# Keys and queries in DRAM with their three parts side by side, read 48 rows at a time

## Chip, cores and metric

One NeuronCore of a Trainium2 chip runs the whole program. The metric is device time in microseconds (us) of one execution; three runs of the kernel before are given. The profile is one more execution, recorded by the hardware profiler.

## The reference

Two layers of an attention block and a dense block over 2048 rows of 512 features, in float32:

```python
B, S, D, H = 1, 2048, 512, 32        # head size 16; dense width F = 1792
def _A_ref(x, wqkv, wo):
    qkv = transpose((x @ wqkv).reshape(B, S, 3, H, Dh), 2, 0, 3, 1, 4)
    q, k, v = qkv[0], qkv[1], qkv[2]
    scores = einsum("bhqd,bhkd->bhqk", q, k) * (Dh ** -0.5)
    p = softmax(scores, axis=-1)
    return transpose(einsum("bhqk,bhkd->bhqd", p, v), 0, 2, 1, 3).reshape(B, S, D) @ wo
def _B_ref(x, w1, b1, w2):            # dense, Mish, dense
    h = einsum("bsd,df->bsf", x, w1) + b1
    return einsum("bsf,fd->bsd", h * tanh(softplus(h)), w2)
x = x + _A_ref(layernorm(x), wqkv, wo)
x = x + _B_ref(layernorm(x), w1, b1, w2)      # and both lines once more
```

## The kernel before

Every float32 number that goes into a matmul is carried as two float32r parts, a high one (`th`, index 0) and a low one (`tl`, index 1), and a product is three matmuls: high by high, high by low, low by high.

**Projections.** `qkv` (L470) goes through a list `order` of tiles (m, c): m is one of 8 blocks of 128 output rows (0 to 3 queries, 4 to 7 keys), c one of 4 chunks of 512 tokens. The tile is 12 matmuls (L164 to L166, or L159 for the first two) into a PSUM bank of the tag "s", of which there are three. `evict` (L488) then splits it: ScalarE writes the high part to the buffer `pt` (L151), VectorE the low part (L152), and one DMA issued on ScalarE's queue (L491) stores both parts, 512 KB, to the DRAM tensor `scr[m]`, laid out [part, row, token]. `pt` has the tag "raw" with three buffers. In layer 0 the tag is shared with freshly loaded weights. Values come after 22 tiles of queries and keys in layer 0 and after 16 in layer 1: `va` tiles, also in the PSUM tag "s", go through ScalarE to one half of `vst` (L537), and a DMA on SyncE's queue (SP, L538) stores them to `vscr`. Both halves are used in turn, so the third value tile waits for the first store.

**A head's operands.** Attention works on eight groups of four heads. A group's two `ks` and two `qs` buffers each hold two heads, at partitions 0 and 64. One head takes 48 rows, which make the three products in one matmul: for keys the 16 rows of the high part twice and those of the low part (`K_PARTS`), for queries high, low, high (`Q_PARTS`). Two further rows hold ones (keys, L244) and the negative row maximum (queries, L337). `prep_qk` (L232) fills the 48 rows with three DMAs of 16 rows each (L251), all on SP's queue, which issues in order. For group 0 it is called twice in `qkv`: for the columns 0 to 1535 when the third chunks of m = 0 and 4 are stored, and for the last 512 columns (the edge) when the fourth chunks are. For later groups it is a generator, which `run` (L420) advances by one DMA at each of the attention's steps, from the group before.

**Attention.** `run` interleaves score matmuls (`sp`, L355), exponentials on ScalarE (L357), products with the values (`pv`, L402), and, 22 steps ahead, the row maxima: matmuls `pm` and `pn` (L275) with VectorE reductions (L293, L308). The first maxima are laid between the value tiles (`some_max`, L479): `pm` takes two heads of the first buffers of `ks` and `qs`, `pn` one head each of the second ones. The order on each engine is settled when the program is built, partly by chains of dependences written in the code (`Order`, L85), elsewhere by a scheduler with a model of the times. An instruction that waits holds back all that stand behind it on its engine.

```python
KROWS = 48
K_PARTS = (0, 0, 1)
Q_PARTS = (0, 1, 0)
```

Of the kernel before, what the change touches and what calls it, by code (L numbers as in the profile page):

```python
# [10 lines left out]
F32 = mybir.dt.float32  # L11
F32R = mybir.dt.float32r
# [7 lines left out]
P = 128  # L20
S, D, H, DH, F = 2048, 512, 32, 16, 1792
NCH = 4
CW = S // NCH
# [10 lines left out]
KROWS = 48  # L34
MROWS = 50
HALF = 64
K_PARTS = (0, 0, 1)
Q_PARTS = (0, 1, 0)
CYCLE = "QvXXvQMXvvXM"
TAIL_START = "QvvRvv"  # L40
TAIL = "WQRvvv"
# [10 lines left out]
def kernel(ctx: ExitStack, tc: tile.TileContext, x, wqkv, wo, w1, b1, w2, out):  # L52
    nc = tc.nc
# [7 lines left out]
    dram = ctx.enter_context(tc.tile_pool(name="dram", bufs=1, space=DRAM))  # L61
# [12 lines left out]
    def b8(shape, dt, name):  # L74
        return blk.tile(shape, dt, tag="blk", name=name)
# [3 lines left out]
    def pbank(tag, name):  # L79
        return ps.tile([P, 512], F32, tag=tag, name=name, bufs=PS_BUFS[tag])  # L80
# [69 lines left out]
    def split_psum(hi, lo, src):  # L150
        nc.scalar.activation(hi, src, AF.Copy)  # L151
        nc.vector.tensor_tensor(lo, src, hi.bitcast(F32), op=ALU.subtract)  # L152
# [8 lines left out]
    def mm3(acc, pairs, first=True, last=True, pe=lambda ins: ins):  # L161
        n = len(pairs)
        for i, (ah, al, bh, bl) in enumerate(pairs):
            pe(nc.tensor.matmul(acc, ah, bh, start=first and i == 0, stop=False))  # L164
            pe(nc.tensor.matmul(acc, ah, bl, start=False, stop=False))  # L165
            pe(nc.tensor.matmul(acc, al, bh, start=False, stop=last and i == n - 1))  # L166
# [49 lines left out]
    class Attention:  # L216
# [15 lines left out]
        def prep_qk(self, g, first=0, last=S):  # L232
            l = self.l
            if g not in self.qk:
                self.qk[g] = [
                    [b8([P, S], F32R, f"{n}s{l}{g}{u}") for u in range(HG // 2)] for n in ("k", "q")
                ]
            for u in range(HG // 2):
                k, q = self.qk[g][0][u], self.qk[g][1][u]
                m, h0 = divmod(g * HG + 2 * u, P // DH)  # L240
                for e in range(2):
                    r0 = e * HALF
                    if first == 0:
                        nc.sync.dma_start(  # L244
                            k[r0 + KROWS : r0 + MROWS].bitcast(F32).rearrange("p (r n) -> p r n", n=256),
                            ones[:, None, :].to_broadcast([MROWS - KROWS, S // 256, 256]),
                        )
                        yield
                    for t, parts, base in ((k, K_PARTS, NCH), (q, Q_PARTS, 0)):
                        for j, a in enumerate(parts):  # L250
                            nc.sync.dma_start(  # L251
                                t[r0 + j * DH : r0 + (j + 1) * DH, first:last].bitcast(F32),
                                self.scr[base + m][a, (h0 + e) * DH : (h0 + e + 1) * DH, first:last].bitcast(F32),
                            )
                            yield

        def prep_v(self, g):
# [206 lines left out]
    def padded(l):  # L464
        vst = b8([P, 2, H, VW], F32, f"vst{l}")
        nc.gpsimd.memset(vst, 0.0)
        nc.gpsimd.memset(vst[:, :, :, DH : DH + 1], 1.0)
        return vst

    def qkv(l, wts, tt, order, before, first=None, vst=None):  # L470
        scr = [dram.tile([2, P, S], F32R, name=f"scr{l}{m}") for m in range(2 * NCH)]
        vscr = dram.tile([NG, P, NKT, HG * VW], F32, name=f"vscr{l}")
        att = Attention(l, scr, vscr)
        if vst is None:
            vst = padded(l)
        chained = False
        done, left = 0, sum(NCH if m == "v" else 1 for m, _ in order[:-1])

        def some_max():  # L479
            nonlocal chained  # L480
            if done == 2 * NCH and left < AHEAD and att.nm < AHEAD:
                chained = True
                att.tick()
                att.max_pair()
                att.max_one()
                att.max_one()

        def evict(m, c, acc):  # L488
            pt = tmp.tile([P, 2, CW], F32R, tag="raw", name=f"pt{l}{m}{c}", bufs=3)
            split_psum(pt[:, 0], pt[:, 1], acc)  # L490
            nc.scalar.dma_start(  # L491
                scr[m][:, :, ts(c, CW)].bitcast(F32).rearrange("a p n -> p a n"), pt.bitcast(F32)
            )

        def put_off(m, c):
            th, tl = tt[c]
            w = wts[m // 2]
            acc = pbank("acc", f"qk{l}{c}{m}")

            def part(k):  # L500
                cols = ts(m % 2, P)
                mm3(
                    acc,
                    [(w[:, 0, k, cols], w[:, 1, k, cols], th[:, k], tl[:, k])],
                    first=k == 0,
                    last=k == KT - 1,
                    pe=att.order,
                )
                if k == KT - 1:
                    evict(m, c, acc)  # L510

            for k in range(KT):
                att.filler.append(lambda k=k: part(k))

        for i, (m, c) in enumerate(order):
            for fn in before.get(i, ()):
                fn()
            if i == len(order) - 1:
                put_off(m, c)
                continue  # L520
            th, tl = tt[c]
            chained = chained or (l == 1 and i >= 11)
            pe = att.order if chained else lambda ins: ins
            if m == "v":
                for t in range(NCH):
                    acc = pbank("s", f"va{l}{c}{t}")
                    mm3(
                        acc,
                        [
                            (th[:, k, ts(t, P)], tl[:, k, ts(t, P)], wts[4 + k // 2][:, 0, k % 2], wts[4 + k // 2][:, 1, k % 2])  # L530
                            for k in range(KT)
                        ],
                        pe=pe,
                    )
                    left -= 1
                    st = vst[:, t % 2]
                    nc.scalar.activation(st[:, :, 0:DH], acc.rearrange("p (h d) -> p h d", d=DH), AF.Copy)  # L537
                    nc.sync.dma_start(  # L538
                        vscr[:, :, c * NCH + t, :].rearrange("g p n -> p g n"),
                        st.rearrange("p (g h) w -> p g (h w)", g=NG),  # L540
                    )
                    some_max()
            else:
                w = wts[m // 2]
                acc = pbank("s", f"qk{l}{c}{m}")
                (mm3_by_kind if l == 0 and i < 2 else mm3)(
                    acc,
                    [(w[:, 0, k, ts(m % 2, P)], w[:, 1, k, ts(m % 2, P)], th[:, k], tl[:, k]) for k in range(KT)],
                    pe=first if first and i < 2 else pe,
                )  # L550
                left -= 1
                evict(m, c, acc)
                if m in (0, 4):
                    done += 1
                    if done >= 2 * NCH - 2 and done % 2 == 0:
                        edge = (NCH - 1) * CW
                        for _ in att.prep_qk(0, *((edge, S) if done == 2 * NCH else (0, edge))):
                            pass
                some_max()
        att.prep_v(0)  # L560
        return att
# [243 lines left out]
    for l in range(2):  # L805
# [7 lines left out]
        order += [("v", c) for c in range(NCH)]  # L813
        order += [(m, c) for m in (2, 6, 3, 7) for c in range(NCH) if (m, c) not in order]
        att = qkv(l, wts, tt, order, before, *((front, vst0) if l == 0 else ()))
        wot, w1t, w2t, x2s, tts = [], [], [], [], {}
        xsrc = x if l == 0 else xs
# [6 lines left out]
        hooks, parts, work = {}, {}, {}  # L824
# [38 lines left out]
        first = norm_steps(x2s[0], f"m{l}0", tts, 0, "s", o)  # L863
# [32 lines left out]
        if l == 0:  # L896
            last = NCH - 1
# [37 lines left out]
```

## Time and profile before

| | us |
|---|---|
| three runs | 3463.2, 3464.74, 3470.34 |
| median | 3464.74 |
| the profiled execution, its own time | 3467.31 |
| span of the profiled execution | 3465.5 |
| TensorE (PE) busy | 3441.9 (99% of the span) |
| VectorE (DVE) busy | 2967.4 (86%) |
| ScalarE (ACT) busy | 2619.8 (76%) |
| moved by DMA | 247.38 MB, mean 71 GB/s |

The span runs from the first to the last recorded instruction; 1.8 us of the execution's own time lie around it. PE busy counts matmuls whose ends are modelled and overlap, so a full share says that PE had always something in hand. "PEld" is the load of weights into PE, "ACTq" and "SPq" are the DMA-issuing instructions of ScalarE and SyncE. "x <- y" in a wait reads: x waited until y was done.

### The profile page before, as it was taken

What the parts mean: (1) busy time and instruction counts of PE and PEld (TensorE: products, weight loads), DVE (VectorE), ACT (ScalarE), POOL (GpSimd) and SP (SyncE); (2) the same over time, 40 slices, a digit from 0 to 9 for tenths busy, and PEclk for the clock granted to TensorE, in tenths of its full rate; (3) what the DMA queues carried; (4) which work ended last, traced back from release to release, by engine and by line L of the source; (5) the groups of instructions that cost most, each with busy time, mean ns of one, the idle gap of its engine ahead of it and who ended that gap; (6) DMA issues with size and microseconds to landing.
All of it is one profiled execution on the core that took longest, in us unless ns stands there. A gap on an engine that the chain in (4) does not pass through costs nothing.

```text
span 3465.5 us, 71149 instructions
## 1 busy us (share of the span) xinstructions
PE 3441.9 (99%) x29075; PEld 1918.7 (55%) x29075; DVE 2967.4 (86%) x4155; ACT 2619.8 (76%) x4865; POOL 282.1 (8%) x329
## 2 busy tenths in 40 slices
PE   9999999999999999999999999999999999999999
PEld 6644444444444445888876444444444444458887
DVE  5699999999999996665537999999999999966554
ACT  3189989889989988356532888898988899874665
POOL 1000000000000000222200000000000000012222
PEclk9999999999999999999999999999999999999999
DMA  7641312213121114500264202112020221154000
GB/s 251 229 105 38 81 41 76 61 54 77 49 58 48 38 55 108 195 13 13 86 192 163 53 15 46 29 33 43 19 56 15 45 37 25 55 134 169 13 13 25
DMA packets 131862, 247.38 MB, mean 71 GB/s; under 512 B 30928, under 2 KB 72400, under 8 KB 116432
## 3 DMA queue, kind: packets, MB, share of 16 engines
q1 hardware_dynamic: 110960, 186.21, 21.2%
q10 hardware_dynamic: 20576, 56.63, 4.2%
q8 instruction: 229, 3.75, 0.5%
q14 instruction: 97, 0.79, 0.1%
HBM read 149.43 MB, written 92.27 MB: 70 GB/s over the span
## 4 chain that ended last, share of the span: by engine, by line
PE 96%; DVE 2%; DMA 1%; ACT 1%; SPq 0%; issue 0%; DVEq 0%; ACTq 0%
PE pv L402 32%; PE sp L355 25%; PE pm L275 8%; PE pn L275 5%; PE h L165 3%; PE h L166 3%; PE h L164 3%; PE mo L164 3%; PE mo L165 3%; PE mo L166 3%; PE qk L164 1%; PE qk L165 1%; PE qk L166 1%; PE va L164 1%; PE va L165 1%; PE va L166 1%
## 5 line engine op out<-in xcount | busy, mean ns | idle before, releaser
L357 ACT ACTIVATE p<-sp 128x512 f32<-128x512 f32 x4040 | 2108.5, 599 | 237.7 <-PE pn L275 144.5
L293 DVE TENSOR_REDUCE mxv<-pm 128x2 f32<-128x1024 f32 x1024 | 1254.8, 1225 | 79.4 <-PE pm L275 79.1
L308 DVE TENSOR_REDUCE mxv<-pn 128x1 f32<-128x512 f32 x2048 | 1318.4, 689 | 3.9 <-PE sp L355 3.7
L355 PE MATMUL sp<-qs,ks 50*128 50x512 f32 x4040 | 1266.1, 445 | 0.0
L402 PE MATMUL pv<-p,va 128*32 128x256 f32 x16384 | 1210.0, 388 | 1.9 <-DVE pt L152 1.9
L355 PEld LDWEIGHTS sp<-qs,ks 50*128 50x128 f32 x4040 | 561.6, 184 | 687.8 <-ACT p L357 620.0
L275 PE MATMUL pn<-ks,qs 48*128 48x512 f32 x2048 | 824.2, 449 | 1.2 <-DVE mxv L308 0.9
L402 PEld LDWEIGHTS pv<-p,va 128*32 128x32 f32 x16384 | 384.8, 108 | 557.8 <-issue 427.6
L275 PE MATMUL pm<-ks,qs 48*128 48x512 f32 x2048 | 435.7, 421 | 1.5 <-DMA ks<-scr 1.5
L275 PEld LDWEIGHTS pn<-ks,qs 48*128 48x128 f32 x2048 | 365.1, 183 | 8.4 <-DVE mxv L308 2.7
L275 PEld LDWEIGHTS pm<-ks,qs 48*128 48x128 f32 x2048 | 192.9, 185 | 63.7 <-issue 7.8
L320 POOL CAST nh<-nm 128x16 fp32r<-128x16 f32 x64 | 12.6, 197 | 2435.0 <-DVE nm L315 2435.0
L666 POOL TENSOR_TENSOR hb<-hb,he 128x512 f32<-128x512 f32 x112 | 148.3, 1324 | 473.1 <-DVE he L663 473.1
L164 PE MATMUL mo<-w,ah 128*128 128x512 f32 x448 | 175.7, 393 | 3.2 <-ACT ah L669 3.0
L165 PE MATMUL mo<-w,ah 128*128 128x512 f32 x448 | 175.2, 391 | 0.0
L166 PE MATMUL h<-thm,w 128*128 128x512 f32 x448 | 175.0, 391 | 0.0
L165 PE MATMUL h<-tlm,w 128*128 128x512 f32 x448 | 174.9, 390 | 0.0
L164 PE MATMUL h<-thm,w 128*128 128x512 f32 x448 | 174.7, 391 | 0.0
L166 PE MATMUL mo<-w,al 128*128 128x512 f32 x448 | 166.9, 392 | 0.0
L668 DVE TENSOR_TENSOR hb<-hb,hr 128x512 f32<-128x512 f32 x112 | 77.3, 691 | 98.9 <-ACT hr L665 73.1
L660 ACT ACTIVATE hb<-h,b1t 128x512 f32<-128x512 f32 x112 | 76.9, 686 | 96.3 <-PE h L166 65.5
L151 ACT ACTIVATE pt<-qk 128x512 fp32r<-128x512 f32 x64 | 38.0, 598 | 146.7 <-PE qk L166 119.9
(133 smaller groups left out, 2595.3 us busy)
## 6 DMA issues: line engine op xcount, KB each, us to landing
scr<-pt ACTq DMA_DIRECT2D x64, 512.0 KB
ks<-scr SPq DMA_DIRECT2D x168, 128.0 KB
qs<-scr SPq DMA_DIRECT2D x168, 128.0 KB
vscr<-vst SPq DMA_DIRECT2D x32, 512.0 KB
va<-vscr SPq DMA_DIRECT2D x16, 1024.0 KB
w<-w1p SPq DMA_DIRECT2D x14, 1024.0 KB
w<-w2p SPq DMA_DIRECT2D x14, 1024.0 KB
raw<-ot SPq DMA_DIRECT2D x256, 32.0 KB
```

The source lines that it names most:

```text
L164: pe(nc.tensor.matmul(acc, ah, bh, start=first and i == 0, stop=False))
L165: pe(nc.tensor.matmul(acc, ah, bl, start=False, stop=False))
L166: pe(nc.tensor.matmul(acc, al, bh, start=False, stop=last and i == n - 1))
L275: nc.tensor.matmul(out, qs[h // 2][rows, q0 : q0 + P], ks[h // 2][rows, ts(c, 512)], start=True, stop=True)
L293: self.order(nc.vector.tensor_reduce(self.mxs[b][:, 0:2, qt, c], pm, axis=AX.X, op=ALU.max))
L308: self.order(nc.vector.tensor_reduce(self.mxs[b][:, h, qt, c : c + 1], pm, axis=AX.X, op=ALU.max))
L355: nc.tensor.matmul(sp, ks[h // 2][rows, ts(kt, P)], qs[h // 2][rows, ts(qb, CW)], start=True, stop=True)
L357: return lambda: self.order(nc.scalar.activation(self.pts[s][:, h], sp, AF.Exp, scale=SCALE))
L402: nc.tensor.matmul(acc[ts(h, VW), cols], va[:, kt, h, :], self.pts[s][:, h, cols], start=kt == 0 and half == 0, stop=kt == NKT - 1, skip_g ...
L660: nc.scalar.activation(hb, acc, AF.Identity, bias=b1t[:, f : f + 1])
L666: nc.gpsimd.tensor_tensor(hb, hb, e, op=ALU.mult)
L668: nc.vector.tensor_tensor(hb, hb, r, op=ALU.mult)
```

## The change

`scr[m]` becomes [row, part, token] with three parts per row, in the order in which a head needs them, so that the 48 rows of a head are adjacent in DRAM. `evict` issues two stores: one of two parts (512 KB, L491 of the changed program) and one of the high part again (256 KB, L492). A head's 48 rows are read in one DMA, except that a whole row of 2048 columns is read in two DMAs of 1024 columns. A generator of one group has 20 steps in place of 28.

```diff
-K_PARTS = (0, 0, 1)
-Q_PARTS = (0, 1, 0)
...
-                    for t, parts, base in ((k, K_PARTS, NCH), (q, Q_PARTS, 0)):
-                        for j, a in enumerate(parts):
-                            nc.sync.dma_start(
-                                t[r0 + j * DH : r0 + (j + 1) * DH, first:last].bitcast(F32),
-                                self.scr[base + m][a, (h0 + e) * DH : (h0 + e + 1) * DH, first:last].bitcast(F32),
-                            )
+                    n = (last - first) // (2 if last - first == S else 1)
+                    for t, base in ((k, NCH), (q, 0)):
+                        rows = self.scr[base + m][(h0 + e) * DH : (h0 + e + 1) * DH].bitcast(F32)
+                        rows = rows.rearrange("d j n -> (d j) n")
+                        for i in range(first, last, n):
+                            nc.sync.dma_start(t[r0 : r0 + KROWS, i : i + n].bitcast(F32), rows[:, i : i + n])
                             yield
...
-        scr = [dram.tile([2, P, S], F32R, name=f"scr{l}{m}") for m in range(2 * NCH)]
+        scr = [dram.tile([P, 3, S], F32R, name=f"scr{l}{m}") for m in range(2 * NCH)]
...
-            nc.scalar.dma_start(
-                scr[m][:, :, ts(c, CW)].bitcast(F32).rearrange("a p n -> p a n"), pt.bitcast(F32)
-            )
+            to = scr[m][:, :, ts(c, CW)].bitcast(F32)
+            both, again = (slice(0, 2), 2) if m < NCH else (slice(1, 3), 0)
+            nc.scalar.dma_start(to[:, both], pt.bitcast(F32))
+            nc.scalar.dma_start(to[:, again], pt[:, 0].bitcast(F32))
```

The scheduler also moves instructions, nearly all of them in the projections of the two layers; in the attention's steady part the order on PE is as before. Line numbers of the changed program are lower by 2 from `prep_qk` to `evict`.

**SP, layer 0, the edge columns of group 0.** Before, 24 reads of 16 rows stand between the last read of the first columns and the first store of values:

```order
L251 DMA qs_590<-scr_200 16x1536 x3
L251 DMA qs_589<-scr_200 16x512 x5
L251 DMA ks_587<-scr_204 16x512 x6
L251 DMA qs_589<-scr_200 16x512
L251 DMA ks_588<-scr_204 16x512 x3
L251 DMA qs_590<-scr_200 16x512 x3
L538 DMA vscr_208<-vst_83 128x8x128 x16
```

And now:

```order
L252 DMA qs_603<-scr_200 48x1536
L252 DMA qs_602<-scr_200 48x512 x2
L252 DMA qs_603<-scr_200 48x512 x2
L252 DMA ks_600<-scr_204 48x512 x2
L252 DMA ks_601<-scr_204 48x512 x2
L537 DMA vscr_208<-vst_83 128x8x128 x16
```

Eight reads have taken the place of the 24, so fewer instructions stand ahead of the first store of values.

**PE, layer 0, the first maxima.** Before, the first `pm` stands after the first matmul of tiles (0, 3) and (4, 3), whose names here are qk_697 and qk_714:

```order
L164 MATMUL qk_697<-thq_559,qkm_91 128x512
L164 MATMUL qk_714<-thq_559,qkm_95 128x512
L275 MATMUL pm_888<-ks_587,qs_589 128x512
L165 MATMUL qk_697<-tlq_560,qkm_91 128x512
L166 MATMUL qk_697<-thq_559,qkm_91 128x512
```

Now it stands behind the last matmul of these two tiles:

```order
L163 MATMUL qk_715<-tlq_572,qkm_95 128x512
L164 MATMUL qk_715<-thq_571,qkm_95 128x512
L273 MATMUL pm_878<-ks_600,qs_602 128x512
L162 MATMUL qk_741<-thq_426,qkm_91 128x512
L163 MATMUL qk_741<-tlq_427,qkm_91 128x512
```

The first `pm` has moved back by 22 matmuls. The first two `pn` went the other way; before, both stand behind the last of the 22 tiles (qk_809), ahead of the first value tile:

```order
L165 MATMUL qk_809<-tlq_560,qkm_95 128x512
L166 MATMUL qk_809<-thq_559,qkm_95 128x512
L275 MATMUL pn_892<-ks_588,qs_590 128x512
L275 MATMUL pn_895<-ks_588,qs_590 128x512
L164 MATMUL va_827<-vm_299,thq_110 128x512
```

Now the first of them stands two tiles earlier, behind tile 20 (qk_760):

```order
L163 MATMUL qk_760<-tlq_572,qkm_91 128x512
L164 MATMUL qk_760<-thq_571,qkm_91 128x512
L273 MATMUL pn_882<-ks_601,qs_603 128x512
L162 MATMUL qk_779<-thq_426,qkm_95 128x512
L163 MATMUL qk_779<-tlq_427,qkm_95 128x512
```

It has moved forward by 24 matmuls, and the second `pn` by 12.

**ACT, layer 0, tiles 21 and 22.** Before, both tiles' high parts are written before the next store (`qkp` is a store of split weights, 1 MB, that layer 1 reads back):

```order
L151 ACTIVATE pt_804<-qk_791 128x512
L151 ACTIVATE pt_822<-qk_809 128x512
L491 DMA scr_205<-pt_804 128x2x512
L133 DMA qkp_195<-qkm_192 128x2048
L491 DMA scr_205<-pt_822 128x2x512
L133 DMA qkp_199<-qkm_196 128x2048
L537 ACTIVATE vst_83<-va_827 128x32x16
```

And now:

```order
L149 ACTIVATE pt_792<-qk_779 128x512
L492 DMA scr_205<-pt_792 128x512
L131 DMA qkp_195<-qkm_192 128x2048
L491 DMA scr_205<-pt_792 128x2x512
L149 ACTIVATE pt_811<-qk_798 128x512
L492 DMA scr_205<-pt_811 128x512
L131 DMA qkp_199<-qkm_196 128x2048
L491 DMA scr_205<-pt_811 128x2x512
L536 ACTIVATE vst_83<-va_817 128x32x16
```

The store of the weights has moved in between the two stores of a tile, and tile 22 stands behind all three of tile 21.

## Rows read from the trace of the kernel before

**Rows 1.** Busy time by stage, with TensorE's clock, DMA share and GB/s last.
```profile
0.00:180.00 180.00, 170.26 (x751) 122.57 (x753) 111.54 (x179) 46.48 (x80) 9.33 (x20) 0.99 0.71 238
180.00:1330.00 1150.00, 1149.06 (x11716) 520.49 (x11716) 1146.34 (x1526) 1032.56 (x1985) 66.78 (x92) 1.00 0.24 60
1740.00:1910.00 170.00, 165.34 (x732) 121.56 (x730) 93.99 (x139) 41.69 (x72) 5.33 (x8) 0.98 0.55 178
1910.00:3050.00 1140.00, 1140.00 (x11652) 515.90 (x11648) 1138.43 (x1516) 1025.23 (x1971) 12.56 (x60) 1.00 0.18 38
```

**Rows 2.** The chain that ended last, by engine.
```profile
PE 96%; DVE 2%; DMA 1%; ACT 1%; SPq 0%; issue 0%; DVEq 0%; ACTq 0%
```

**Rows 3.** Waits of PE from 0 to 180 us (total, times, longest).
```profile
PE va L164 <- ACT vst L537: 1.6, 1, 1.6
PE pm L275 <- DMA ks<-scr: 1.5, 1, 1.5
```

**Rows 4.** Busy time by stretch in the projections of layer 0.
```profile
60.00:66.00 6.00, 6.00 (x30) 4.81 (x28) 2.58 (x4) 1.76 (x5) 0.00 (x0) 1.00 1.02 240
66.00:68.00 2.00, 0.53 (x3) 0.18 (x1) 0.69 (x1) 0.46 (x1) 0.00 (x0) 1.00 0.96 262
68.00:99.00 31.00, 31.00 (x134) 24.54 (x133) 6.38 (x9) 4.57 (x8) 0.00 (x0) 1.00 0.97 333
...
102.00:106.00 4.00, 4.00 (x12) 2.88 (x11) 0.13 (x1) 1.20 (x2) 0.00 (x0) 0.63 0.98 362
```

**Rows 5.** The chain from 20 to 101 us: start, us, what.
```profile
27.93 3.60 DMA scr<-pt
...
60.80 5.54 DMA scr<-pt
...
96.99 0.69 SPq L251
97.81 2.95 DMA vscr<-vst
100.86 0.61 ACT vst L537
```

**Rows 6.** DMA issues of the page: count and KB each.
```profile
scr<-pt ACTq DMA_DIRECT2D x64, 512.0 KB
ks<-scr SPq DMA_DIRECT2D x168, 128.0 KB
```

**Rows 7.** The tensor scr: issue ns (least, median, most) and count.
```profile
L251 SPq DMA_DIRECT2D qs<-scr x216: 302/415/2012, 58.1 to 2859.0; - x108
L251 SPq DMA_DIRECT2D ks<-scr x216: 302/418/1697, 62.5 to 2855.4; - x108
L491 ACTq DMA_DIRECT2D scr<-pt x64: 366/366/687, 20.0 to 1908.9; - x64
```

**Rows 8.** Busy time by stretch: reads alone, then layer 1's projections.
```profile
192.00:195.00 3.00, 3.00 (x36) 1.56 (x36) 3.00 (x5) 2.52 (x6) 0.00 (x0) 1.00 0.91 184
1765.00:1785.00 20.00, 20.00 (x98) 16.38 (x97) 7.71 (x15) 6.26 (x11) 0.55 (x1) 1.00 1.00 302
1785.00:1800.00 15.00, 15.00 (x68) 12.43 (x67) 3.37 (x5) 2.99 (x5) 0.00 (x0) 1.00 0.78 266
```

**Rows 9.** ACT in order of time, 81 to 101 us, idle before in brackets.
```profile
86.12 1.09 ACT L151 ACTIVATE pt<-qk 128x512 fp32r<-128x512 f32 x2 [5.39 <-DMA scr<-pt]
...
100.86 0.60 ACT L537 ACTIVATE vst<-va 128x512 f32<-128x512 f32 x1 [7.96 <-DMA vscr<-vst]
```

**Rows 10.** PE in order of time, the first two pn of layer 0.
```profile
84.92 0.49 PE L275 MATMUL pn<-ks,qs 48*128 48x512 f32 x2
```

**Rows 11.** DVE in order of time, the low part of tile 21.
```profile
86.75 0.69 DVE L152 TENSOR_TENSOR pt<-qk,pt 128x512 fp32r<-128x512 f32 x1 [5.29 <-ACT pt L151]
```

**Rows 12.** ACT in order of time, layer 1's projections.
```profile
1766.33 0.60 ACT L151 ACTIVATE pt<-qk 128x512 fp32r<-128x512 f32 x1 [3.47 <-DMA scr<-pt]
...
1775.11 0.60 ACT L151 ACTIVATE pt<-qk 128x512 fp32r<-128x512 f32 x1 [2.10 <-DMA ks<-scr]
```

## Prediction

> **What bounds the kernel.** First the busy time by stage, to see where time can be won at all. In the two long stretches of attention, 2290 us together, PE is busy for 1149.06 of 1150 us and 1140.00 of 1140 us, and the DMA engines for 0.24 and 0.18 of the time [rows 1]. In the two stretches of projections PE is idle for 180 - 170.26 = 9.7 us and 170 - 165.34 = 4.7 us, and the DMA share is 0.71 and 0.55 [rows 1]. The chain of work that ended last says the same: 96% PE, 1% DMA [rows 2]. So the kernel is bound by PE's own work, which the change leaves alone, and the change can win only a part of the 14 us in which PE stands idle in the projections, or add to them.
>
> Then PE's waits in layer 0's projections. Two of them hang on the traffic that the change touches: 1.5 us of the first `pm` on its keys, and 1.6 us of a value tile on `vst` [rows 3]. The busy time by stretch shows the state of the DMA engines there: 1.02 busy from 60 to 66 us, 0.97 from 68 to 99 us, at 240 and 333 GB/s [rows 4]. The reader is to see that from 60 us on the DMA engines are full while PE runs nearly without gaps: every byte added here delays another byte, and the question is whose.
>
> **The change part by part.**
>
> *Steady attention.* The reads go from 432 to 256: 24 per group become 16 (14 groups, each layer's first one left out), and the first groups' 48 per layer become 16. At 415 ns [rows 7] that takes 176 x 0.415 = 73 us off SP's queue. The bytes read are the same. PE has 0.9 us of idle time in 2290 us, none of it for these reads [rows 1], so this counts 0. Its cover is the early start of a generator, which runs an eighth of a group ahead; without it the first maxima of each group would wait for its reads.
>
> *The second store.* 64 tiles store 256 KB more each [rows 6], at 333 GB/s [rows 4] 0.79 us of all DMA engines per tile (1.09 us at 240, 0.72 us at 362 GB/s). The 64 added issues on ACT's queue, 366 ns each [rows 7], are 23 us for both layers; ACT's work in 0 to 180 us is 46.48 us [rows 1], so they stand beside idle time and count 0; exposed they would be 23 us.
>
> *Layer 0, before 60 us.* One store stands on the chain, 3.60 us at 27.93 us, since its buffer is awaited by the next tile [rows 5]. The high part's store can start before the low part is made, so the delay lies between 0 and 1.1 us; I take **+0.8**, the price at the rate of the fuller stretch.
>
> *The first `pm`.* It moves back 22 matmuls; at 31.00/134 = 0.231 us [rows 4] that is 5.1 us. Its reads can be late by the longer stores of tiles (0, 2) and (4, 2), 2 x 0.79 = 1.6 us, which is less. The wait of 1.5 us [rows 3] goes: **-1.5**, at worst 0.
>
> *The wait for `vst`.* The third value tile's copy waited 7.96 us for a store of values [rows 9] that SP issued at 97.81 us, right behind the last edge read [rows 5]. With 8 edge reads for 24, SP comes to it 16 x 0.415 = 6.6 us earlier, when all else stays. PE then doesn't wait the 1.6 us [rows 3]. [...] Together **-2.8**, at worst 0.
>
> *Tiles 19 to 22.* This is where the added bytes bite. The high part of tile 21 waited 5.39 us for a store to give a `pt` buffer back [rows 9], and its low part was done at 86.75 + 0.69 = 87.44 us [rows 11]. PE needs that PSUM bank for the second value tile, which it reaches at 84.92 us plus two `pn` plus 12 matmuls, 14 x 0.231 = 3.2 us: 88.2 us [rows 10]. The margin is 0.7 us. The longer stores of tiles 17 to 20 add 4 x 0.79 = 3.2 us, and the store of weights that now lies between a tile's two stores, 1 MB, another 3.1 us to a buffer's return. So PE waits between 0 (if the weights' stores alone give way) and 6.3 - 0.7 = 5.6 us, plus 1.2 us of slow clock. I take 3.2 - 0.7 = 2.5 and the clock: **+3.7**, since a store's own bytes can't be avoided, while the weights are spread over all stores.
>
> *The first `pn`.* It moves forward 24 matmuls, 5.5 us, to 79.4 us, and needs the last of the first columns' reads. These are 24 x 96 KB (16 rows of 1536 columns of 4 bytes) = 2.36 MB. Three back-to-back reads of 16 rows moved 184 GB/s and kept the engines 0.91 busy [rows 8]; at that rate the reads take 12.8 us from 58.1 us [rows 7], to 70.9 us; if the stores take half of the engines, to 83.7 us. So the wait is between 0 and 4.3 us, with the clock 5.5 us. The middle, 77.3 us, is in time: **0**.
>
> *What merging does to the rate of a read.* The row above has reads of 16 rows at 184 GB/s with nothing beside them; nothing in it says that 48 rows at once go faster, and I take the same rate. [...]
>
> *Layer 1.* From 1765 to 1785 us the DMA engines are 1.00 busy at 302 GB/s, PE makes 98/12 = 8 tiles without a gap [rows 8], and ACT waits 3.47 and 2.10 us for transfers [rows 12]. The added stores are 8 x 0.87 = 6.9 us there (256 KB at 302 GB/s). ACT's lag would reach 2.1 + 6.9 = 9.0 us, and PE can go ahead by two more banks, 2 x 12 x 0.231 = 5.5 us: at most 3.5 us of wait and 1.2 us of clock. At least it is 0, since the reads beside them are not needed soon and from 1785 us on the share is 0.78 [rows 8]. I take **+1.0**.
>
> **Sum.** 0.8 - 1.5 - 2.8 + 3.7 + 0 + 1.0 = +1.2 us on the profiled execution's 3467.3 us. The median of the runs shown is 2.6 us below it, so 3464.7 + 1.2 = 3466 us. The best ends give -4.3 (3460.4), the worst 18.1 us. A measurement of this kernel can tell about 0.2%, 7 us, from no change.
>
> **Rivals.**
>
> *All gain.* The added bytes push only the weights' stores back, which nobody awaits before layer 1: 0 - 1.5 - 2.8 = -4.3, 3460.4 us. For it: the engines are 0.78 busy in the latter part of layer 1 and PE stands still only twice in layer 0. Against it: the margin of 0.7 us at tile 21.
>
> *Slower: the longer store holds the `pt` buffers.* A tile's buffer comes back only when both stores have landed, so ACT falls behind, and PE stops for want of a bank. It decides from a lag of 0.7 us at tile 21 in layer 0, and of 5.5 us in layer 1. With both at their upper ends: 0.8 - 1.5 - 2.8 + 6.8 + 0 + 4.7 = +8.0, 3472.7 us. For it: an engine share of about 1 in both stretches, and the weights' store between the two. Against it: ACT's waits in layer 1 have not reached PE so far.
>
> *The early `pn` waits.* With 5.5 us for it and the other terms as forecast: +6.7, 3471.4 us. Against it: eight reads are issued faster than 24.
>
> [...]
>
> That the change doesn't do what it says is out: SP's order has 8 edge reads where it had 24.
>
> **Chances.** Forecast 0.47, all gain 0.17, held buffers 0.20, early `pn` 0.08, double rate 0.08. Neither gaining case reaches 7 us by itself; with the spread of the runs, 7 us, about a quarter of them might: faster 0.07. Slower takes three quarters of the held buffers and a part of the early `pn`: 0.18. Same 0.75. The range goes from 3458 us (the gaining cases and the 1.5 us by which the lowest run lies under the median) to 3476 us (held buffers and half of a `pn` wait): it leaves out the runs in which several bad ends meet.
>
> **What would show it.** In the changed profile: PE's wait of `pm` on `ks` and of a value tile on `vst` gone; a wait of PE's second or third value tile on the low part of tile 21 or 22; the steady stretches at the same PE time; the DMA share near 1 for longer, and 16.8 MB more written. Wrong would be a change of over 2 us in the steady stretches, no more engine time per tile, or a new wait of PE on `qs` or `ks`.

## The result, and the profile after

The changed kernel takes 3472.39 us (median of 14 runs, 3469.28 to 3477.28), the kernel before 3464.31 us (14 runs, 3461.42 to 3470.83). The ratio is 1.0020, 95% interval 1.0014 to 1.0027: 8 us slower, 6.4 above the forecast of 3466 us and inside its range. The profiled execution took 3471.81 us, its span is 3470.0 us.

Busy time by stretch, kernel before (columns as in [rows 1]; the stretches are cut finer than there):

```profile
20.00:60.00 40.00, 37.92 (x186) 30.67 (x185) 28.86 (x55) 17.36 (x32) 2.67 (x3) 1.00 0.56 203
60.00:100.00 40.00, 38.43 (x168) 29.83 (x166) 9.95 (x15) 6.78 (x13) 0.00 (x0) 1.00 0.98 316
100.00:140.00 40.00, 38.49 (x163) 26.60 (x164) 24.79 (x31) 7.78 (x13) 0.00 (x0) 0.96 0.71 226
140.00:180.00 40.00, 39.41 (x174) 26.19 (x175) 32.74 (x46) 8.26 (x14) 0.42 (x2) 1.00 0.49 173
```

The same view of the changed kernel; its long stretches answer to [rows 1], and the last line is a piece of the attention in which reads of 48 rows run with hardly anything beside them, as in [rows 8]:

```profile
20.00:60.00 40.00, 35.51 (x158) 28.27 (x158) 27.18 (x52) 15.67 (x28) 2.51 (x3) 0.91 0.69 252
60.00:100.00 40.00, 38.59 (x166) 29.22 (x164) 11.72 (x18) 7.44 (x13) 0.00 (x0) 1.00 1.00 342
100.00:140.00 40.00, 36.36 (x154) 25.34 (x156) 19.35 (x24) 7.06 (x12) 0.00 (x0) 0.96 0.80 270
140.00:180.00 40.00, 40.00 (x180) 27.37 (x180) 31.12 (x42) 6.84 (x12) 0.41 (x2) 1.00 0.59 206
180.00:1330.00 1150.00, 1148.46 (x11678) 521.45 (x11674) 1146.65 (x1527) 1029.40 (x1979) 66.77 (x92) 1.00 0.22 62
...
1740.00:1910.00 170.00, 165.31 (x737) 122.46 (x736) 94.17 (x142) 42.37 (x74) 6.87 (x9) 1.00 0.65 228
1910.00:3050.00 1140.00, 1139.06 (x11632) 515.57 (x11636) 1138.27 (x1516) 1024.95 (x1972) 12.54 (x60) 1.00 0.16 38
...
237.00:240.00 3.00, 3.00 (x36) 1.28 (x34) 3.00 (x5) 2.64 (x6) 0.00 (x0) 1.00 1.06 186
```

The number of matmuls behind PE's busy time says where PE falls behind: 28 fewer from 20 to 60 us (158 for 186), 2 fewer from 60 to 100, 9 fewer from 100 to 140, 6 more from 140 to 180. That is 33 in all; at 40.00/180 = 0.222 us, the distance in the stretch where PE never stops, some 7 us before the attention begins.

For layer 1 the same stretch of time isn't the same work, since the changed kernel comes to it 7 us later. The view of its query and key tiles gives the start of the first and of the last matmul of one line, in the kernel before, the changed kernel and e10 (an experiment below, which has the stores of before):

```profile
L166 PE MATMUL qk<-thq,qk x128: 387/389/628, 1733.7 to 1906.4; 128*128 128x512 f32 x128
...
L164 PE MATMUL qk<-thq,qk x128: 388/389/402, 1740.5 to 1911.1; 128*128 128x512 f32 x128
...
L166 PE MATMUL qk<-thq,qk x128: 387/390/476, 1731.1 to 1901.4; 128*128 128x512 f32 x128
```

That is 172.7, 170.6 and 170.3 us. The kernel before had a lower clock there in this execution (0.98 [rows 1]); at a clock of 1.00, as the changed kernel and e10 had it, the changed kernel takes 0.3 us more than e10, which shows no loss.

PE's waits from 0 to 185 us, changed kernel; they answer to [rows 3]:

```profile
PE va L162 <- ACT vst L536: 3.9, 2, 2.0
PE qk L162 <- ACT thq L149: 3.6, 1, 3.6
...
PE va L162 <- DVE pt L150: 1.2, 1, 1.2
```

The wait of `pm` on `ks` is gone. The wait on `vst`, which was to go, has grown from 1.6 to 3.9 us. `thq` is ScalarE's copy of a transposed tile of normed input, which the next tiles multiply; its wait is new.

ACT in order of time in the changed kernel ("ACTq" issues a store); the row at 109.41 us answers to the second of [rows 9]:

```profile
27.35 0.38 ACTq L491 DMA_DIRECT2D scr<-pt  x1
...
32.78 0.60 ACT L149 ACTIVATE pt<-qk 128x512 fp32r<-128x512 f32 x1 [2.20 <-DMA scr<-pt]
...
35.09 0.60 ACT L149 ACTIVATE thq<-tpq 128x512 fp32r<-128x512 f32 x1 [0.41 <-ACT pt L149]
...
100.95 1.09 ACT L536 ACTIVATE vst<-va 128x512 f32<-128x512 f32 x2 [4.96 <-DMA ks<-scr]
109.41 0.60 ACT L536 ACTIVATE vst<-va 128x512 f32<-128x512 f32 x1 [7.37 <-DMA vscr<-vst]
```

The chain that ended last, same kernel; it answers to [rows 5]:

```profile
27.35 6.65 DMA scr<-pt
34.07 0.61 ACT pt L149
35.09 0.53 ACT thq L149
...
84.85 8.71 DMA scr<-pt
...
93.93 6.47 DMA ks<-scr
...
100.95 0.61 ACT vst L536
101.61 7.70 DMA vscr<-vst
```

Read together: the stores of tiles 2 and 3 take up to 6.65 us where the latter took 3.60 [rows 5]; on ACT the next two tiles wait for their buffers, the first for 2.20 us; `thq` stands behind them in ACT's order (PE has its transposes done at 31.70 + 1.04 = 32.74 us, ACT comes to it at 35.09), and PE waits 3.6 us for it. After that wait the granted clock was low: from 36 to 43 us PE makes 17 matmuls at a clock of 0.51, in the next 7 us 36 at 1.00.

```profile
36.00:43.00 7.00, 6.56 (x17) 4.90 (x18) 6.25 (x14) 2.38 (x5) 0.61 (x1) 0.51 0.72 278
43.00:50.00 7.00, 7.00 (x36) 5.76 (x36) 2.94 (x6) 2.71 (x5) 0.40 (x1) 1.00 0.62 237
```

Later the same happens to the edge reads. In the kernel before, the store that they follow on the chain took 4.66 us:

```profile
72.32 4.66 DMA scr<-pt
```

In the changed kernel the one that the last of them follow takes 8.71 us, and SP issues these reads only then:

```profile
93.58 3.80 SPq L252 DMA_DIRECT2D ks<-scr  x4
```

SP is through with them at 97.38 us, against 97.68 before [rows 5]: 8 reads for 24 have won next to nothing. The first store of values starts at 101.61 us instead of 97.81, and lands after 7.70 us instead of 2.95.

The page shows the added bytes: 109.05 MB written, 16.8 MB more than before, as 64 x 256 KB make.

### The profile page after: what moved, and what is told of

Read it like the earlier page. It is cut to its first block, busy times and chain, and to the rows that moved or that the text cites. A ratio compares the mean times of both kernels' runs of the same rounds, so it can differ in the third digit from the quotient of the medians.

```text
span 3470.0 us, 71130 instructions
## 1 busy us (share of the span) xinstructions
PE 3441.1 (99%) x29075; PEld 1917.1 (55%) x29075; DVE 2966.2 (85%) x4155; ACT 2619.6 (75%) x4865; POOL 281.8 (8%) x329
## 3 DMA queue, kind: packets, MB, share of 16 engines
HBM read 149.43 MB, written 109.05 MB: 74 GB/s over the span
## 4 chain that ended last, share of the span: by engine, by line
PE 95%; DMA 2%; DVE 2%; ACT 1%; issue 0%; SPq 0%; ACTq 0%; DVEq 0%
PE pv L400 32%; PE sp L353 25%; PE pm L273 8%; PE pn L273 4%; PE h L164 3%; PE h L163 3%; PE h L162 3%; PE mo L162 3%; PE mo L163 3%; PE mo L164 3%; PE qk L162 1%; DMA scr<-pt 1%; PE qk L163 1%; PE qk L164 1%; PE va L162 1%; PE va L164 1%
## 5 line engine op out<-in xcount | busy, mean ns | idle before, releaser
L291 DVE TENSOR_REDUCE mxv<-pm 128x2 f32<-128x1024 f32 x1024 | 1241.8, 1213 | 78.0 <-PE pm L273 78.0
```

The costliest lines, as they stand in the source:

```text
L291: self.order(nc.vector.tensor_reduce(self.mxs[b][:, 0:2, qt, c], pm, axis=AX.X, op=ALU.max))
```

## The experiments

Each run also lists the mean clock that TensorE was granted. It differs from run to run of one kernel, and the time with it: 106 runs of the kernel before, listed beside the experiments, average 3461.6 us at a clock of 1.000 (14 runs), 3463.3 at 0.999 (29), 3466.0 at 0.998 (41), 3469.1 at 0.997 (17) and 3471.1 at 0.996 (4; one run had 0.995). A straight line through them falls by 2.5 us per thousandth. So the table has, beside the ratio to the kernel before, the mean time of the runs at a clock of 0.998 and 0.999. Differences in these columns are those that no clock explains, called stalls here. They are rough: the clock is listed to a thousandth, which is worth 2.5 us, and most cells have few runs. This view was formed after the runs; the expectations speak of the times as a whole.

| kernel | median us | ratio, 95% | mean clock | at 0.998 (runs) | at 0.999 (runs) |
|---|---|---|---|---|---|
| before | 3464.3 to 3465.9 | 1 | 0.9983 | 3466.0 (41) | 3463.3 (29) |
| the change | 3472.39 | 1.0020 [1.0014, 1.0027] | 0.9979 | 3472.1 (4) | 3469.8 (4) |
| e1, 256 KB more per tile | 3481.72 | 1.0043 [1.0029, 1.0057] | 0.9968 | 3480.3 (1) | - |
| e7, 128 KB more per tile | 3472.13 | 1.0021 [1.0012, 1.0030] | 0.9983 | 3472.5 (6) | 3471.0 (4) |
| e2, three parts, reads of 16 rows | 3478.28 | 1.0033 [1.0022, 1.0045] | 0.9976 | 3476.0 (4) | 3474.2 (1) |
| e3, two parts, reads of 48 rows | 3467.99 | 1.0003 [0.9994, 1.0012] | 0.9977 | 3467.3 (3) | 3464.1 (3) |
| e8, whole rows in one read | 3470.90 | 1.0020 [1.0011, 1.0029] | 0.9977 | 3471.6 (6) | 3469.6 (2) |
| e5, change, weights later | 3472.17 | 1.0021 [1.0013, 1.0030] | 0.9967 | 3469.1 (3) | - |
| e6, before, weights later | 3465.03 | 1.0002 [0.9993, 1.0010] | 0.9983 | 3465.2 (4) | 3463.9 (5) |
| e9, change, weights in attention | 3466.22 | 0.9999 [0.9991, 1.0008] | 0.9984 | 3467.3 (5) | 3464.8 (6) |
| e10, before, weights in attention | 3461.27 | 0.9988 [0.9979, 0.9996] | 0.9994 | 3466.1 (1) | 3461.8 (5) |
| e11, e9 and four stores copied later | 3465.79 | 1.0001 [0.9992, 1.0010] | 0.9979 | 3466.3 (4) | 3461.7 (3) |
| e12, e10 and four stores more | 3465.98 | 1.0003 [0.9994, 1.0013] | 0.9985 | 3467.5 (3) | 3465.2 (5) |

At a like clock the change costs 6.1 to 6.5 us; its runs' lower mean clock makes about another 1.

### Bytes or reads?

**e1**: the kernel before, with 256 KB more stored per tile, to a tensor that nobody reads.

```diff
+        extra = [dram.tile([P, S], F32R, name=f"extra{l}{m}") for m in range(2 * NCH)]
...
+            nc.scalar.dma_start(extra[m][:, ts(c, CW)].bitcast(F32), pt[:, 0].bitcast(F32))
```

> The kernel before, with one edit: each tile's high part is stored a second time, 256 KB, to a DRAM tensor that nobody reads. Reads and the layout of scr stay. Theory A (the added bytes, and the later return of the pt buffers, cost the time): as slow as the changed kernel, 3470 to 3474 us, and PE makes about 160 matmuls from 20 to 60 us as there, where it made 186 before. Theory B (the merged 48-row reads, or the new row pitch, cost it): as before, 3462 to 3466 us, 186 matmuls.

**e2**: the change, its reads again three of 16 rows.

```diff
-                        for i in range(first, last, n):
-                            nc.sync.dma_start(t[r0 : r0 + KROWS, i : i + n].bitcast(F32), rows[:, i : i + n])
+                        for j in range(3):
+                            nc.sync.dma_start(
+                                t[r0 + j * DH : r0 + (j + 1) * DH, first:last].bitcast(F32),
+                                self.scr[base + m][(h0 + e) * DH : (h0 + e + 1) * DH, j, first:last].bitcast(F32),
+                            )
```

> The change's layout and its two stores, but a head's 48 rows are read in three transfers of 16 rows as before. Theory A (added bytes): 3470 to 3474 us, about 160 matmuls on PE from 20 to 60 us, and the wait of the first pm on ks (1.5 us before) absent because pm stands later. Theory B (merged reads): 3462 to 3466 us. If merged reads give something back that the stores take, this run is slower than the changed kernel by 2 us or more.

**e3**: reads of 48 rows, but `scr[m]` with two parts per row and the one store of before. The 48 rows that a read takes are then not those of its head, so the scores are of other numbers.

```diff
+                        rows = self.scr[base + m].bitcast(F32).rearrange("d j n -> (d j) n")
+                        at = min((h0 + e) * 2 * DH, 2 * P - KROWS)
+                        rows = rows[at : at + KROWS]
...
+        scr = [dram.tile([P, 2, S], F32R, name=f"scr{l}{m}") for m in range(2 * NCH)]
...
+            nc.scalar.dma_start(scr[m][0:P, :, ts(c, CW)].bitcast(F32), pt.bitcast(F32))
```

> The merged reads without the second store: rows lie side by side in two parts, one store of 512 KB per tile, and 48 adjacent rows are read in one transfer (or two halves). The 48 rows are then not the right ones, so the scores are of other rows; the work is the same. Theory A (added bytes): not slower than before, 3460 to 3465 us, 186 matmuls from 20 to 60 us. Theory B (merged reads or their layout): 3470 to 3474 us. The difference to the kernel before is what merging alone gives: I expect 0 to -3 us, from the first pm and from vst.

Measured: e1 is 17 us slower than before, e2 14 us, e3 the same as before. From 20 to 60 us PE makes 158, 157 and 186 matmuls, as Theory A had it. The times are all above those expected, e1 by 8 us, e2 by 4, e3 by 3; e3's lower clock makes a part of that, and at a like clock it is 1 us above the kernel before. The added bytes cost, the merged reads don't. The reads do give something back beside the added stores: 3478.3 - 3472.4 = 6 us by the medians, about 4 at a clock of 0.998. Without the stores they give nothing. PE's waits from 0 to 185 us in e3:

```profile
PE va L162 <- DVE pt L150: 1.6, 1, 1.6
...
PE pn L274 <- DMA qs<-scr: 1.2, 1, 1.2
...
PE va L162 <- ACT vst L534: 0.4, 1, 0.4
```

The wait of `pm` is gone and that on `vst` is down from 1.6 to 0.4 us, as the prediction had it for eight edge reads, but a wait of `pn` on a read and one of a value tile on tile 21's low part stand in their place.

**e8**: the change with a whole row of 2048 columns in one read.

```diff
-                    n = (last - first) // (2 if last - first == S else 1)
+                    n = last - first
```

> The changed kernel with a whole row of 2048 columns read in one transfer, not in two halves; the first group's reads are the same. All theories: the steady stretches are bound by PE, so as the changed kernel, 3469 to 3475 us. A difference of over 3 us would say that the length of a read on SP's queue matters in the steady stretches.

It takes what the change takes, 1.5 us less by the medians and 0.2 to 0.5 at a like clock; no gain or loss by the halves is shown.

**e7**: e1 with half the bytes.

```diff
+            nc.scalar.dma_start(extra[m][:, ts(c, CW // 2)].bitcast(F32), pt[:, 0, 0 : CW // 2].bitcast(F32))
```

> The kernel before with half of the dose: a second store of 128 KB per tile to a tensor that nobody reads. PE's order in the first 60 us is that of the kernel before, not that of the changed one. If the cost goes with the bytes, half of the 17 us that 256 KB cost: 3471 to 3474 us, and 170 to 175 matmuls on PE from 20 to 60 us. If it is a matter of a wait that passes a limit and then drops the clock: 3464 to 3468 us and 184 to 187 matmuls, since the early wait stays short. If it was the scheduler's new order (Theory E), the first 60 us are as before too, and so this run leaves E open there unless it is slow.

0, 128 and 256 KB per tile cost 0, 7 and 17 us by the medians, 0, 6.5 and 14.3 at a clock of 0.998 (one run of e1): about with the bytes. The time is the one expected for that; the matmuls from 20 to 60 us, 179, lie between the two expectations. PE's order there is that of the kernel before, so a new order of the scheduler isn't what costs e7 its 7 us. In e7 the first 60 us stay almost whole and the loss is that of the value tiles (179 and 149 matmuls; 186 and 163 before):

```profile
20.00:60.00 40.00, 36.74 (x179) 29.71 (x178) 29.05 (x55) 17.01 (x30) 2.79 (x3) 1.00 0.66 241
...
100.00:140.00 40.00, 35.78 (x149) 24.49 (x148) 20.64 (x26) 6.58 (x11) 0.00 (x0) 0.91 0.69 220
```

### Is it the buffers?

**e4**: the change with four buffers of the tag "raw" in place of three. The room is taken from three tags of the dense block, so only the first 180 us are read.

```diff
-T_BUFS = {"he": 1, "hr": 1}
+T_BUFS = {"he": 1, "hr": 1, "hb": 1, "al": 1, "ah": 1}
...
-            pt = tmp.tile([P, 2, CW], F32R, tag="raw", name=f"pt{l}{m}{c}", bufs=3)
+            pt = tmp.tile([P, 2, CW], F32R, tag="raw", name=f"pt{l}{m}{c}", bufs=4)
```

> The changed kernel with four buffers of the tag raw (pt and fresh weights) in place of three; the room is taken from three work tags of the dense block, which get one buffer each, so the dense block and the whole time are slower and only the first 180 us are read. Theory A, in the form that the buffers' later return stops ACT and with it PE: PE makes 180 or more matmuls from 20 to 60 us (158 in the changed kernel), and the 3.6 us wait on thq goes. Theory C (the DMA engines are simply full, buffers don't matter): 160 or fewer.

```profile
20.00:60.00 40.00, 37.39 (x175) 29.90 (x175) 28.96 (x54) 16.82 (x30) 2.99 (x3) 0.96 0.78 276
...
100.00:140.00 40.00, 38.31 (x165) 26.17 (x163) 21.97 (x28) 7.13 (x12) 0.00 (x0) 0.96 0.75 244
```

Between the two expectations: 175 matmuls lie between 158 and 186, and the wait for `thq` is 2.0 us. A fourth buffer takes away over half of the early loss. This is one execution.

### What the stores of weights do

**e5**, **e6**: the six 1 MB stores of split weights, which ACT issued behind tiles 19 to 24, issued behind the value tiles, in the change (e5) and in the kernel before (e6).

```diff
-        at(19 + n, lambda n=n: stores[n]())
+        at(26 + n, lambda n=n: stores[n]())
```

> The changed kernel with the six stores of split weights (1 MB each) moved behind the value tiles, so that none stands between a tile's two stores or competes before the first store of values; the order of the tiles and of PE is the same. Theory D (in the stretch from 84 to 110 us a tile's last store waits behind the weights' store, the edge reads behind that, and the first store of values behind these): the two waits of value tiles on vst (3.9 us) and the 1.2 us on pt go, with one slow-clock stretch of 3.4 us, so 5 to 7 us faster than the changed kernel, 3465 to 3468 us; the 3.6 us wait on thq near 36 us stays. Theory C (the added 256 KB stores alone fill the engines there): less than 2 us of gain, 3470 us or more.

> The same move in the kernel before. Theory D says that its wait of 1.6 us on vst and the slow clock behind it come from the same stores: 2 to 4 us faster than before, 3460 to 3463 us. Theory C: no difference, since before has no added stores and the wait comes from the 24 edge reads that SP issues one by one.

Two stretches of e5:

```profile
100.00:140.00 40.00, 40.00 (x179) 27.40 (x178) 25.36 (x32) 6.75 (x12) 0.00 (x0) 1.00 0.50 150
140.00:180.00 40.00, 37.55 (x162) 25.15 (x160) 31.22 (x44) 5.98 (x10) 0.42 (x2) 0.97 0.97 366
```

The waits on `vst` are gone, and PE is whole from 100 to 140 us. But the stores now fill the DMA engines (0.97) at the start of the attention, where PE loses 2.45 us and the clock is 0.97. The median doesn't move: at a clock of 0.998 e5 is 3.0 us faster than the change, and its mean clock is lower. In e6 too PE is whole from 100 to 140 us (40.00) and loses 1.56 us from 140 to 180, with the engines 0.87 busy; its time stays. So both times came out as Theory C had it, while the traces show the place that Theory D named.

**e9**, **e10**: the same six stores in the first steps of the attention, where the engines are 0.24 busy [rows 1], one every four steps.

```diff
-    for n in range(6):
-        at(19 + n, lambda n=n: stores[n]())
...
+            for n in range(6):
+                hooks[2 + 4 * n] = lambda n=n: stores[n]()
```

> The change, with the six 1 MB stores of split weights issued during the first steps of layer 0's attention, one every four steps, in place of behind the tiles 19 to 24. [...] The early wait for thq, 3 to 3.6 us, stays. Time 3466 to 3470 us. Rival E (6 MB of stores in the attention collide with the reads of the next group's operands): the steady stretch from 180 to 1330 us loses 3 us or more of PE time, and the time stays at 3472 us.

> The kernel before, with the same move of the six stores of weights. Theory D: the wait of a value tile on vst (1.6 us) and the slow clock behind it are gone and nothing is given back from 140 to 180 us, so 2 to 4 us faster than before: 3460 to 3463 us. Rival E: no difference or slower, with PE time lost from 180 to 1330 us.

Busy time by stretch in e9:

```profile
20.00:60.00 40.00, 35.22 (x160) 28.29 (x159) 27.39 (x52) 15.91 (x28) 2.35 (x3) 0.91 0.69 253
...
100.00:140.00 40.00, 40.00 (x180) 27.45 (x178) 24.35 (x31) 7.11 (x12) 0.00 (x0) 1.00 0.52 158
...
180.00:1330.00 1150.00, 1149.06 (x11730) 521.50 (x11731) 1147.41 (x1528) 1033.26 (x1986) 66.78 (x92) 1.00 0.23 66
```

And in e10:

```profile
20.00:60.00 40.00, 36.76 (x172) 29.57 (x172) 27.61 (x54) 16.67 (x30) 2.76 (x3) 0.96 0.54 199
...
100.00:140.00 40.00, 40.00 (x179) 27.47 (x178) 25.96 (x33) 6.57 (x11) 0.00 (x0) 1.00 0.50 150
140.00:180.00 40.00, 39.40 (x174) 26.00 (x173) 32.31 (x46) 8.95 (x16) 0.42 (x2) 1.00 0.49 177
```

Both came out as Theory D had it: PE is busy for 40.00 of 40 us from 100 to 140 us and for 39.40 from 140 to 180, and both times lie in the ranges expected. With the weights out of the way the change costs nothing against the kernel before, and the kernel before gains 4 us: e10, at 3461.27 us, is faster than both. At a like clock its gain is 1.5 us; the larger part is that 5 of its 11 runs had a clock of 1.000, against 14 of 106 before, and 3 of the 23 listed beside it. e9 against e10 is what the change costs beside the weights: 5.0 us by the medians, 3.0 at a clock of 0.999.

### What is left: the first tiles

**e11**: e9, with the second store of the first four tiles off ACT's queue. SP copies the high part within DRAM. The copies stand eight tiles later in the program; SP, which runs ahead, issues them between 23 and 40 us.

```diff
+            if (l, c) == (0, 0) and m in (0, 4, 1, 5):
+                again_later.append(lambda: nc.sync.dma_start(to[:, again], to[:, both.start]))
+            else:
+                nc.scalar.dma_start(to[:, again], pt[:, 0].bitcast(F32))
...
+            if i in (8, 9, 10, 11) and again_later:
+                again_later.pop(0)()
```

> The change with the weights' stores in the attention, and beside it the second store of the first four tiles taken off ACT's queue: the high part is copied from DRAM to DRAM by SP's queue some five tiles later (the bytes stay and are read once more, but no pt buffer is held by them and nothing of them lies before the first four tiles' own stores have landed). [...] Rival G (the loss is of the bytes, whenever they are moved before 60 us, or of the order of the instructions): 165 matmuls or fewer, and 3465 to 3468 us.

**e12**: e10, with e1's added store for the first four tiles alone.

```diff
+            if (l, c) == (0, 0) and m in (0, 4, 1, 5):
+                nc.scalar.dma_start(extra[m][:, ts(c, CW)].bitcast(F32), pt[:, 0].bitcast(F32))
```

> The kernel before with the weights' stores in the attention (3461.3 us), and beside it a store of another 256 KB, to a tensor that nobody reads, for the first four tiles of layer 0 alone: 1 of the 16.8 MB that the change adds. Theory F (what is left of the loss, once the weights are out of the way, is made by the second stores of the first four tiles): the wait for thq is 3 us or more, PE makes 160 to 170 matmuls from 20 to 60 us (172 without these stores), and the time is 3464 to 3466 us. Rival G (what is left is spread over all 64 tiles, or is of layer 1): the time stays at 3461 to 3462 us.

From 20 to 60 us in e11:

```profile
20.00:60.00 40.00, 36.95 (x173) 29.72 (x172) 28.59 (x54) 16.83 (x30) 2.44 (x3) 0.96 0.78 274
```

In e12, the same stretch:

```profile
20.00:60.00 40.00, 35.04 (x171) 28.18 (x170) 27.95 (x54) 16.67 (x30) 2.45 (x3) 1.00 0.61 221
```

And the matmul that waits for `thq`, in order of time, with PE's idle time ahead of it in brackets: the kernel before, the change, e9, e10, e11 and e12:

```profile
33.25 0.73 PE L164 MATMUL qk<-thq,qkm 128*128 128x512 f32 x2 [0.84 <-ACT thq L151]
...
36.31 1.22 PE L162 MATMUL qk<-thq,qkm 128*128 128x512 f32 x2 [3.57 <-ACT thq L149]
...
36.56 1.22 PE L162 MATMUL qk<-thq,qkm 128*128 128x512 f32 x2 [3.02 <-ACT thq L149]
...
34.54 0.73 PE L164 MATMUL qk<-thq,qkm 128*128 128x512 f32 x2 [0.84 <-ACT thq L151]
...
34.53 0.73 PE L162 MATMUL qk<-thq,qkm 128*128 128x512 f32 x2 [1.81 <-ACT thq L149]
...
36.47 0.73 PE L164 MATMUL qk<-thq,qkm 128*128 128x512 f32 x2 [2.46 <-ACT thq L151]
```

PE starts this matmul at the same time in e10 and e11, and 1.9 to 2.0 us later in e12 and e9: the four stores put on make the delay, and taken off ACT's queue they take it away, though e11 moves their bytes in the same 40 us (engines 0.78 busy). The order of instructions can't be the cause, for PE and ACT compute in the same order in all six up to here. Behind this matmul e9 and e12 have PE's order of the change, e10 and e11 that of the kernel before up to the first `pm`; whether that order has a part in what follows, no run separates.

e12's time says Theory F: 1 MB in four stores costs 4.7 us by the medians and 3.4 at a clock of 0.999, about the 5.0 and 3.0 us between e9 and e10. Its profile says so in part: the wait is 2.5 us where 3 were expected, and PE is idle for 4.96 us from 20 to 60 us against e10's 3.24, but 171 matmuls are hardly fewer than e10's 172, since the clock fell in e10's execution (0.96) and not in e12's. e11's profile says Theory F (173 matmuls for e9's 160, and a wait of 1.8 us for e9's 3.0, though the clock, 0.96, fell all the same), its median says Rival G. At a clock of 0.999 it takes 3461.7 us, as e10; its mean clock is lower, 0.9979. So the stall of these four stores is shown from both sides: about 2 us in single traces, 3.0 to 3.4 in the times, by few runs at each clock. Why e11's runs were granted less clock is open.

## Why the prediction was right, and where it failed

The time lay in the range, 6.4 us above the point. It is at the rival of the held buffers (3472.7 us), and that rival's mechanism is what the trace shows; but its parts were laid elsewhere, and that its figure is met within 0.3 us is luck: it has 4.7 us in layer 1, where no loss is shown, and 0.8 before 60 us, where some 5 were lost.

- *Steady attention, 0:* right. PE is busy for 1148.46 of 1150 and 1139.06 of 1140 us, for 1149.06 and 1140.00.
- *The first `pm`, -1.5:* right, the wait is gone.
- *The first `pn`, 0:* right in the change. e3 shows how near it was: there a `pn` waited 1.2 us.
- *Layer 1, +1.0:* no new wait, and 170.6 us for e10's 170.3 at the same clock. Too high by nearly the whole of it.
- *Before 60 us, +0.8:* **mis-sized**. It measured 2 to 3 us of stall (in the traces 3.1 between the change and the kernel before, 2.0 and 1.9 between e9, e12 and e10; 3.0 and 3.4 in their times at a like clock) and, in the profiled execution, some 2 more of clock. The step priced the longer transfer alone, between 0 and 1.1 us. A store on that chain took 6.65 us, 3 more than before, with the engines 0.69 busy for 0.56; and behind the buffer on ACT stood `thq`, which PE needs at once. The question "what is queued behind the waiting instruction on its engine" was asked for tile 21 and not here.
- *The wait for `vst`, -2.8:* **wrong in sign**, +2.3 us in place of it (3.9 for 1.6). The step took SP's edge reads as the last that held the first store of values. With the stores of before, in e3, that held: the wait is 0.4 us. In the change neither half did. The 6.6 us that SP was to win came to 0.3 (97.38 us for 97.68), since its edge reads waited for a store of 8.71 us; "when all else stays" was the condition that failed. And the last to come was ACT: the copies into `vst` stand behind the stores of tiles 21 and 22 and of the weights on ACT's queue, at 100.95 us, and their store then ran 7.70 us. By the chain ACT itself was held there until an edge read of `ks` had landed; why, the profile doesn't show. Of the -2.8, 1.2 us were for the clock behind the wait, and the +3.7 and the upper ends for the first `pn` and layer 1 have the same 1.2: an estimate from the 12 matmuls that PE made there in 4.00 us at a mean clock of 0.63 [rows 4], where 12 x 0.231 = 2.8 us would do. The changed kernel has such a stretch behind its longer wait: 12 matmuls in 4.00 us, from 110.5 to 114.5 us, at a clock of 0.57.
- *Tiles 19 to 22, +3.7:* the place is right, since moving the weights frees it (e9, e5). The wait at tile 21 itself was 1.2 us; the rest came as the waits on `vst`. Priced as one sum, these two terms made +0.9 us. Measured at a like clock: the move of the weights gives the change 6.5 - 1.5 = 5.0 us (0.999: 3469.8 to 3464.8) and the kernel before 3463.3 - 3461.8 = 1.5, so this place costs 3.5 us more than before.
- *Merged reads at an unchanged rate:* right. In the line of 237 to 240 us above, reads of 48 rows move 186 GB/s with the engines full; reads of 16 rows moved 184 at 0.91 [rows 8]. The rate hardly rose with the rows of a read, and e3 shows no gain in time either. A double rate, to which the prediction gave 0.08, no run shows.

The terms found, 3.0 for the first tiles and 3.5 for the place of the weights and values, make 6.5 us, and 6.1 to 6.5 is what the change costs at a like clock. They come from the same four kernels' times, so their sum is no check of its own; that the first is about 3 is checked by e12 (3.4, without what the change gains at `pm`), and by the traces only as far as 2 to 3.

## What to carry to other kernels

Price added bytes by whose buffer they hold and what stands behind its owner in the queue, not by their own transfer time: 1 MB in four early stores cost 4.7 us, all 16.8 MB cost 8 (3.4 and 6.5 at a like clock). Merged reads didn't pay for the added bytes here, with the engines 0.69 to 1.00 busy from 20 to 140 us: they gave back 6 us by the medians, about 4 at a like clock (e2 against the change), and the change lost 8 all the same. Moving large transfers that nobody awaits out of a full stretch paid where they went to one that was nearly idle (e10, engines 0.24 busy, 4 us by the medians) and not where they filled it (e6, 0.87, no gain). When differences are a few microseconds, compare runs at the same granted clock too.

## What the runs showed of the hardware

The spread of the runs of the kernel before, whose means at one clock go from 3461.6 to 3471.1 us, follows the clock that TensorE was granted, 2.5 us per thousandth of its mean. The changed kernel lost time to PE's wait of 3.6 us and again to the clock after it, 0.51 from 36 to 43 us and 0.91 in the mean from 20 to 60 us. The link is not fixed: with e12's wait of 2.5 us the mean from 20 to 60 us was 1.00, and in e10, where PE's longest wait in that stretch was 1.5 us, 0.96.
